# The first MLP's second product, issued two slices behind its first product

## The chip, the cores and the metric

The kernel runs on one core of one Trainium2 chip. The metric is the device time of one execution in microseconds (us). A core has five engines that run their own instruction queues in order: TensorE (PE; its weight loads are listed apart as PEld), VectorE (DVE), ScalarE (ACT), GpSimd (POOL) and SyncE (SP, which here issues the DMAs). They meet only through semaphores.

## The reference

Attention reads between `x` (8 batches, 8 heads, 512 rows, 64 columns) and 32 state rows per head, in both directions; the result, 4352 rows of 512, goes through two MLPs, 512 to 2048 to 512, one after the other.

```python
def _moe_ref(x, w_in, w_out, alpha):
    h = x @ w_in
    g = np.maximum(h, 0.0) + alpha * np.minimum(h, 0.0)
    return (g @ w_out).astype(np.float32)

def _moe2_ref(x, w_in, w_out):
    h = x @ w_in
    g = h - np.tanh(h)
    return (g @ w_out).astype(np.float32)
```

## The kernel before, in words

Every fp32 operand of a product is kept as two parts, a high one and the remainder, and a product is three matmuls (high x high, high x low, low x high). The program is written out by hand: the order of the calls in the Python code is the order in each engine's queue.

The first MLP takes the rows in nine blocks: block 0 to block 7 are the batches (512 rows each), block 8 holds the 256 state rows. Its hidden dimension of 2048 is cut into 16 slices of 128 (`f`). A *visit* is one slice of one block. The visits go: block 0, slices 0 to 7; block 1, all 16; block 0, slices 8 to 15; then blocks 2, 3, 4, 5, 6, the state block, and block 7. Within a visit:

- `emit_h` (L614) is the first product: 12 matmuls of 512 columns in block 0, 12 of 256 in the state block, 6 of 512 in the others (there it works from projected states, `ps_p`, L406, two projections a visit in parts of the run). It writes a PSUM bank `ps_h`.
- The activation is four instructions that alternate between two engines: ACT `t` (L621), DVE on `ps_h` (L622), ACT `g` high part (L623), DVE `g` low part (L627). `g` and `t` have two buffers each.
- `emit_o` (L642) is the second product of the slice before (`pend`): 12 matmuls into four PSUM banks `acc` that stay open over a block. At a block's last slice `finish` copies them out (ACT L667, DVE L669).

Other work is hung into a visit at five places by a table `plan`: "early" (after the first product), "gap" (after the start of the activation), "mid", "late" (after the second product) and "end". That is the attention of the next blocks, the projections, the conversion of the first MLP's weights (visits of block 0 and 1; DVE L114, L116, L119, ACT L111, L123 and casts, POOL), the combination of the second MLP's weights (`c_` names, blocks 3 to the state block), and loads. Four PSUM banks `ps_a` are shared by `ps_h`, the projections and the attention's transposes and scores; the pool gives out a bank whose tile has had its last reader. After the first MLP come the second's two products (L832, L1013).

Of the kernel before, what the change touches and what calls it, by code (L numbers as in the profile page):

```python
# [13 lines left out]
F32R = mybir.dt.float32r  # L14
# [8 lines left out]
P = 128  # L23
# [12 lines left out]
def attention_and_two_mlps(ctx, tc, x, state, w1_in, w1_out, alpha, w2_in, w2_out, out):  # L36
    nc = tc.nc
    B, H, S, D = x.shape
# [17 lines left out]
    work = tc.alloc_tile_pool(name="work", bufs=2)  # L56
# [39 lines left out]
    def w_out(f, part):  # L96
        return WO[f // FQ][:, part, f % FQ, :]
# [245 lines left out]
    def lead(b):  # L343
        return b if b % 2 or b == B - 1 else b - 1
# [259 lines left out]
    def emit_h(blk, n, f):  # L604
        ps = ps_a.tile([P, S], F32, tag="a", name="ps_h")
        if 0 < blk < B:
            col = slice(f % FQ * P, (f % FQ + 1) * P)
            pairs = [([PW[blk, f // FQ, g][i][:, col] for i in range(2)], X[0, blk, g]) for g in range(NG)]
        else:
            w = [WS[f][:, i] if blk else w_in(f, i) for i in range(2)]  # L610
            pairs = [([w[i][:, cc, :] for i in range(2)], X[0, blk, cc]) for cc in range(NCC)]
        for k, (w, xt) in enumerate(pairs):
            for m, (i, j) in enumerate(TERMS):
                nc.tensor.matmul(ps[:, :n], lhsT=w[i], rhs=xt[:, j, :n], start=(k == 0 and m == 0),  # L614
                                 stop=(k == len(pairs) - 1 and m == 2))
        return ps[:, :n]

    def act_a(n, f, ph):
        g = work.tile([P, 2, S], F32R, tag="g", name="g")
        t = work.tile([P, S], F32, tag="t", name="t")[:, :n]  # L620
        nc.scalar.mul(t, ph, slope[:, f:f + 1])  # L621
        nc.vector.scalar_tensor_tensor(ph, ph, sign[:, f:f + 1], t, op0=ALU.mult, op1=ALU.max)  # L622
        nc.scalar.mul(g[:, 0, :n], ph, sign[:, f:f + 1])  # L623
        return g

    def act_b(n, f, ph, g):
        nc.vector.scalar_tensor_tensor(g[:, 1, :n], ph, sign[:, f:f + 1], g[:, 0, :n].bitcast(F32),  # L627
                                       op0=ALU.mult, op1=ALU.subtract)

    accs = {}  # L630

    def emit_o(blk, n, f, g):
        w = [w_out(f, i) for i in range(2)]
        first, last = f == 0, f == NF - 1
        if blk == 0:
            first, last = first or f == NF // 2, last or f == NF // 2 - 1
        if first:
            accs[blk] = [ps_acc.tile([P, S], F32, tag="acc", name="acc") for _ in range(NCC)]
        acc = accs[blk]
        for t in range(NCC):  # L640
            for k, (i, j) in enumerate(TERMS):
                nc.tensor.matmul(acc[t][:, :n], lhsT=w[i][:, t * P:(t + 1) * P], rhs=g[:, j, :n],  # L642
                                 start=(first and k == 0), stop=(last and k == 2))
        if last:
            finish(blk, n, acc)
# [9 lines left out]
    def finish(blk, n, acc):  # L655
        for t, a in enumerate(acc):
            if blk == 0 and half_sum:
                y = half_sum[t]
                nc.vector.tensor_tensor(y, a, y, op=ALU.add)
                stores.append((blk, t, y))  # L660
                continue
            if t < 2:
                y = work.tile([P, S], F32, tag="y", name="y")[:, :n]
            else:
                y = work.tile([P, S], F32, tag="sc" if t == 2 else "at", name="y", bufs=1)[:, :n]
            if t % 2 == 0:
                nc.scalar.copy(y, a[:, :n])  # L667
            else:
                nc.vector.tensor_copy(y, a[:, :n])  # L669
            stores.append((blk, t, y))  # L670
# [3 lines left out]
    def store():  # L674
        for blk, t, y in stores:
            nc.sync.dma_start(out=y_dram[blk][t], in_=y)
        stores.clear()
# [366 lines left out]
    def at(i, f, when, *todo):  # L1044
        plan.setdefault((i, f, when), []).extend(todo)
# [28 lines left out]
    with tc.manual_schedule():  # L1074
# [12 lines left out]
        def halves(i, f, *places):  # L1087
            for k, place in enumerate(places):
                at(i, f, place, (conv_step_a, conv_step_b)[k % 2])
# [25 lines left out]
        for b in range(2, B):  # L1115
            for g in range(NG):
                i, f = (0, 0) if b == 2 else (b - 2, 6 + 7 * g) if b == lead(b) else (b - 2, 1 + g)
# [18 lines left out]
        for i, (blk, n) in enumerate(seq):  # L1136
            if 1 < blk < B:
                for q in range(NF // FQ):
                    at(*((i - 1 if i > 2 else 0, 12, "late") if q == 0 else (i, 4 * q - 4 + (i == 2 and q == 1), "early")),
                       partial(load_parts, blk, q))  # L1140

        for i, (blk, n) in enumerate(seq):
# [50 lines left out]

        for f in range(NF // 2):
            halves(0, f, "late", "end")
        pend = None
        visits = [(0, f) for f in range(NF // 2)] + [(1, f) for f in range(NF)] + [(0, f) for f in range(NF // 2, NF)]
        visits += [(i, f) for i in range(2, len(seq)) for f in range(NF)]
        for i, f in visits:
            blk, n = seq[i]  # L1200
            ph = emit_h(blk, n, f)
            for z in plan.get((i, f, "early"), ()):
                z()
            g = act_a(n, f, ph)
            for z in plan.get((i, f, "gap"), ()):
                z()
            if i < B:
                act_b(n, f, ph, g)
            for z in plan.get((i, f, "mid"), ()):
                z()  # L1210
            if i == B:
                act_b(n, f, ph, g)
            if pend:
                emit_o(*pend)
            for z in plan.get((i, f, "late"), ()):
                z()
            pend = (blk, n, f, g)
            for z in plan.get((i, f, "end"), ()):
                z()
            store()  # L1220
        emit_o(*pend)
        store()

        w_outs.release()
# [116 lines left out]
```

## Time and profile before

| what | value |
|---|---|
| median of 3 runs | 1490.14 us (1488.76 to 1491.17) |
| the profiled execution | 1494.99 us, its span 1493.2 us |
| PE busy | 1418.0 us (95%) |
| DVE, ACT, POOL busy | 988.2 (66%), 728.8 (49%), 533.8 us (36%) |
| mean granted TensorE clock | 0.984 |
| L642 matmuls, 1728 | 420.7 us busy, 24.1 us idle before them, 14.8 of it ended by ACT g L623 |
| L614 matmuls, 600 with projected states | 156.9 us busy |

A row of a timeline reads: start, duration, engine, line, operation, output<-input, count, and in brackets the idle time before it with what ended it. A matmul's duration overlaps the next one's, so the step from one group to the next is shorter than its busy time. The first MLP's visits run from 27.66 us to about 803 us of the span. By the starts of the first products, block 1 begins at 105.28, block 2 at 261.39, block 3 at 362.39, the state block at 676.08 and block 7 at 736.84 us.

### The profile page before, as it was taken

The page shows a single profiled execution, that of the slowest core. Times are in us where ns is not written, and L with a number is a line of the kernel's source. Part 1 is how long each engine was busy: PE and PEld are TensorE (multiplying, and loading weights), DVE is VectorE, ACT ScalarE, POOL GpSimd, SP SyncE. Part 2 cuts the span into 40 slices and gives each one's busy share as a digit, 9 for nine tenths or more (in the row PEclk, how much of TensorE's full clock was granted, in tenths as well). Part 3 has the DMA queues.
Part 4 walks back from the last instruction along what each step waited for, and adds up shares of the span by engine and source line. Part 5 has one row for each costly group of instructions (what it writes and reads, how often), then busy time and mean ns, then how long its engine had stood idle before and what let it go on. Part 6 is the DMA issues. An engine that isn't in the chain of part 4 may idle for free.

```text
span 1493.2 us, 22867 instructions
## 1 busy us (share of the span) xinstructions
PE 1418.0 (95%) x8188; PEld 1191.7 (80%) x8188; DVE 988.2 (66%) x1430; ACT 728.8 (49%) x1322; POOL 533.8 (36%) x414
## 2 busy tenths in 40 slices
PE   5869899999899999999999999999999999999998
PEld 2647678777677677778887787877978999999998
DVE  7988755566677576666345555566348698878884
ACT  4656543444555555555334545455245354444443
POOL 2645310000354444446100122222017486666662
PEclk9989999999999999999999999999999999999999
DMA  6446537986677786769855765462986834444321
GB/s 162 133 136 176 142 110 278 314 259 177 185 186 227 205 249 193 227 184 300 247 167 198 250 232 195 141 255 92 318 309 231 309 124 135 141 135 142 135 86 36
DMA packets 227906, 288.12 MB, mean 193 GB/s; under 512 B 57808, under 2 KB 133584, under 8 KB 226768
## 3 DMA queue, kind: packets, MB, share of 16 engines
q1 hardware_dynamic: 227792, 286.66, 60.1%
q8 instruction: 64, 1.05, 0.3%
q14 instruction: 50, 0.41, 0.1%
HBM read 166.54 MB, written 117.96 MB: 191 GB/s over the span
## 4 chain that ended last, share of the span: by engine, by line
PE 70%; DVE 8%; DMA 6%; ACT 4%; issue 3%; SPq 1%; POOL 1%; DVEq 0%; ACTq 0%; POOLq 0%
PE ps_m L1013 21%; PE ps_m L832 17%; PE acc L642 16%; PE ps_h L614 9%; PE ps_p L406 2%; DVE ps_h L622 2%; PE ps_m L897 2%; DVE g L627 2%; DMA gt<-g 1%; DMA c_raw<-in_moe_w_in 1%; ACT g L623 1%; ACT t L621 1%; DMA g<-t 1%; DVE c L849 1%; PE ps_s L503 1%
## 5 line engine op out<-in xcount | busy, mean ns | idle before, releaser
L642 PE MATMUL acc<-g,wo 128*128 128x512 f32 (+1 forms) x1728 | 420.7, 391 | 24.1 <-ACT g L623 14.8
L642 PEld LDWEIGHTS acc<-g,wo 128*128 128x128 f32 x1728 | 314.5, 192 | 108.8 <-ACT g L623 20.0
L1013 PE MATMUL ps_m<-wp,s 128*128 128x256 f32 x2856 | 343.9, 283 | 2.1 <-ACT e L996 2.0
L1013 PEld LDWEIGHTS ps_m<-wp,s 128*128 128x128 f32 x2856 | 342.7, 191 | 3.4 <-ACT e L996 2.3
L832 PE MATMUL ps_m<-x,ch 128*128 128x512 f32 x1344 | 312.4, 394 | 6.3 <-DVE c L849 4.5
L832 PEld LDWEIGHTS ps_m<-x,ch 128*128 128x128 f32 x1344 | 251.9, 188 | 66.4 <-DVE c L849 6.4
L958 DVE TENSOR_TENSOR s<-gt,s 128x512 fp32r<-128x512 f32 (+1 forms) x216 | 221.1, 1075 | 44.5 <-ACT s L974 43.5
L622 DVE SCALAR_TENSOR_TENSOR ps_h<-ps_h,sign,t 128x512 f32<-128x512 f32 (+1 forms) x144 | 104.7, 727 | 145.4 <-ACT t L621 144.8
L623 ACT ACTIVATE g<-ps_h,sign 128x512 fp32r<-128x512 f32 (+1 forms) x144 | 95.8, 665 | 163.6 <-DVE ps_h L622 163.6
L974 ACT CAST s<-gt 128x512 fp32r<-128x512 f32 (+1 forms) x216 | 120.4, 597 | 89.3 <-PE ps_m L1013 37.4
L614 PE MATMUL ps_h<-x,pw 128*128 128x512 f32 x600 | 156.9, 397 | 0.0
L627 DVE SCALAR_TENSOR_TENSOR g<-ps_h,sign,g 128x512 fp32r<-128x512 f32 (+1 forms) x144 | 102.6, 712 | 60.9 <-ACT g L623 57.9
L621 ACT ACTIVATE t<-ps_h,slope 128x512 f32<-128x512 f32 (+1 forms) x144 | 95.7, 665 | 87.6 <-PE ps_h L614 86.9
L843 POOL TENSOR_TENSOR t<-c,t 128x512 f32<-128x512 f32 x32 | 41.7, 1302 | 249.7 <-ACT t L842 226.4
L614 PEld LDWEIGHTS ps_h<-x,pw 128*128 128x128 f32 x600 | 111.0, 189 | 24.2
L236 POOL TENSOR_TENSOR c_q<-c_m,c_q 128x512 int32<-128x512 int32 x32 | 42.1, 1316 | 241.4 <-ACT c_q L123 191.8
L842 ACT ACTIVATE t<-c 128x512 f32<-128x512 f32 x96 | 60.5, 632 | 124.0 <-DVE c L849 112.1
L849 DVE TENSOR_TENSOR c<-ps_m,c 128x512 f32<-128x512 f32 x96 | 64.8, 685 | 56.4 <-PE ps_m L832 47.8
L263 POOL TENSOR_TENSOR c_o<-c_q,c_o 128x512 fp32r<-128x512 f32 (+1 forms) x48 | 54.4, 1134 | 109.7 <-ACT c_o L261 109.7
L843 DVE TENSOR_TENSOR t<-c,t 128x512 f32<-128x512 f32 x64 | 53.9, 843 | 46.6 <-ACT t L842 44.4
L940 POOL TENSOR_TENSOR s<-gt,gt 128x512 f32<-128x512 f32 (+1 forms) x36 | 54.3, 1517 | 85.0 <-DMA gt<-g 83.6
L166 POOL TENSOR_TENSOR cq<-cm,cq 128x512 int32<-128x512 int32 x32 | 41.9, 1311 | 102.3 <-DVE cm L119 64.7
(142 smaller groups left out, 1659.0 us busy)
## 6 DMA issues: line engine op xcount, KB each, us to landing
g<-t SPq DMA_DIRECT2D x128, 256.0 KB, 2.3
gt<-g SPq DMA_DIRECT2D x64, 512.0 KB, 4.9
wc<-c_o SPq DMA_DIRECT2D x112, 256.0 KB, 3.2
ch<-wc SPq DMA_DIRECT2D x56, 512.0 KB, 6.9
pw<-pw SPq DMA_DIRECT2D x96, 256.0 KB, 5.2
wp<-wc SPq DMA_DIRECT2D x28, 512.0 KB, 7.8
xr<-in_x SPq DMA_DIRECT2D x64, 128.0 KB, 3.3
raw<-in_moe_w_in SPq DMA_DIRECT2D x16, 512.0 KB, 3.8
```

Source lines behind the costliest of these rows:

```text
L614: nc.tensor.matmul(ps[:, :n], lhsT=w[i], rhs=xt[:, j, :n], start=(k == 0 and m == 0), stop=(k == len(pairs) - 1 and m == 2))
L621: nc.scalar.mul(t, ph, slope[:, f:f + 1])
L622: nc.vector.scalar_tensor_tensor(ph, ph, sign[:, f:f + 1], t, op0=ALU.mult, op1=ALU.max)
L623: nc.scalar.mul(g[:, 0, :n], ph, sign[:, f:f + 1])
L627: nc.vector.scalar_tensor_tensor(g[:, 1, :n], ph, sign[:, f:f + 1], g[:, 0, :n].bitcast(F32), op0=ALU.mult, op1=ALU.subtract)
L642: nc.tensor.matmul(acc[t][:, :n], lhsT=w[i][:, t * P:(t + 1) * P], rhs=g[:, j, :n], start=(first and k == 0), stop=(last and k == 2))
L832: nc.tensor.matmul(b, lhsT=w[p][:, cc], rhs=XT[key, i][cc][:, q], start=(i not in GOES_ON and cc == k == 0), stop=(cc == 1 and k == 2), sk ...
L843: eng.tensor_tensor(t, h, t, op=ALU.subtract)
L849: nc.vector.tensor_tensor(h, ps[j, i], h, op=ALU.add)
L958: nc.vector.tensor_tensor(made[k - 1][:, 1], src, made[k - 1][:, 0].bitcast(F32), op=ALU.subtract)
L974: nc.scalar.copy(made[k][:, 0], source(blk, i, jj))
L1013: nc.tensor.matmul(dst[:, t * HW:(t + 1) * HW], lhsT=s[:, p, r, t * P:(t + 1) * P], rhs=w[:, q], start=first, stop=(jj == NJ // 2 - 1 and ...
```

## The change

`emit_o` now runs for the slice before the last one: `pend` is a queue, and in visit f the second product of slice f-2 is issued. The allocation of `g` and its high part move out of `act_a` into `act_b`, behind "gap", "mid" and the second product. `g` keeps two buffers, so g(f) takes the buffer that the second product of f-2, issued just before, has read. Line numbers shift by one: L621, L622, L623, L627 of before are L620, L621, L625, L626 after. One load of projected states of block 2 moves from visit 1 to visit 2 of that block.

```diff
     def act_a(n, f, ph):
-        g = work.tile([P, 2, S], F32R, tag="g", name="g")
         t = work.tile([P, S], F32, tag="t", name="t")[:, :n]
         nc.scalar.mul(t, ph, slope[:, f:f + 1])
         nc.vector.scalar_tensor_tensor(ph, ph, sign[:, f:f + 1], t, op0=ALU.mult, op1=ALU.max)
+
+    def act_b(n, f, ph):
+        g = work.tile([P, 2, S], F32R, tag="g", name="g")
         nc.scalar.mul(g[:, 0, :n], ph, sign[:, f:f + 1])
-        return g
-
-    def act_b(n, f, ph, g):
         nc.vector.scalar_tensor_tensor(g[:, 1, :n], ph, sign[:, f:f + 1], g[:, 0, :n].bitcast(F32),
                                        op0=ALU.mult, op1=ALU.subtract)
+        return g
...
-                    at(*((i - 1 if i > 2 else 0, 12, "late") if q == 0 else (i, 4 * q - 4 + (i == 2 and q == 1), "early")),
+                    at(*((i - 1 if i > 2 else 0, 12, "late") if q == 0 else (i, 4 * q - 4 + 2 * (i == 2 and q == 1), "early")),
...
-            g = act_a(n, f, ph)
+            act_a(n, f, ph)
             for z in plan.get((i, f, "gap"), ()):
                 z()
-            if i < B:
-                act_b(n, f, ph, g)
             for z in plan.get((i, f, "mid"), ()):
                 z()
-            if i == B:
-                act_b(n, f, ph, g)
-            if pend:
-                emit_o(*pend)
+
+            if len(pend) == 2:
+                emit_o(*pend.popleft())
+            pend.append((blk, n, f, act_b(n, f, ph)))
             for z in plan.get((i, f, "late"), ()):
                 z()
-            pend = (blk, n, f, g)
             for z in plan.get((i, f, "end"), ()):
                 z()
             store()
-        emit_o(*pend)
+        while pend:
+            emit_o(*pend.popleft())
```

On PE, near the end of block 6, before: a first product, the second product of the slice before it (`g_6395` is made from `ps_h_6388`, the next rows show), a first product.

```order
L614 MATMUL ps_h_6431<-x0_6_0_5355,pw_6197 128x512 x3
L614 MATMUL ps_h_6431<-x0_6_1_5690,pw_6200 128x512 x3
L642 MATMUL acc_5867<-g_6395,wo3_903 128x512 x3
L642 MATMUL acc_5868<-g_6395,wo3_903 128x512 x3
L642 MATMUL acc_5869<-g_6395,wo3_903 128x512 x3
L642 MATMUL acc_5870<-g_6395,wo3_903 128x512 x3
L614 MATMUL ps_h_6467<-x0_6_0_5355,pw_6197 128x512 x3
```

The same visit on PE now: the second product takes `g_6364`, which is made from `ps_h_6311`, the slice before `ps_h_6376`.

```order
L614 MATMUL ps_h_6419<-x0_6_0_5343,pw_6185 128x512 x3
L614 MATMUL ps_h_6419<-x0_6_1_5678,pw_6188 128x512 x3
L642 MATMUL acc_5892<-g_6364,wo2_1255 128x512 x3
L642 MATMUL acc_5893<-g_6364,wo2_1255 128x512 x3
L642 MATMUL acc_5894<-g_6364,wo2_1255 128x512 x3
L642 MATMUL acc_5895<-g_6364,wo2_1255 128x512 x3
L614 MATMUL ps_h_6455<-x0_6_0_5343,pw_6185 128x512 x3
```

The products themselves and their number are unchanged; the second is one slice further back.

On ACT, the two visits before that one, before: `t`, the high part `g`, then other work. What each instruction waits for stands in brackets.

```order
L621 ACTIVATE t_6331<-ps_h_6323,slope_92 128x512 [waits PE_49,Activation_49]
L623 ACTIVATE g_6330<-ps_h_6323,sign_91 128x512 [waits DVE_49]
L123 ACTIVATE c_q_6364<-c_raw_6188 128x512
L336 CAST x0_7_1_6379<-at_6335 128x512 [waits DVE_49]
L261 CAST c_o_6386<-c_s_6275 128x512 [waits DMAHW7_49,Pool_49]
L621 ACTIVATE t_6396<-ps_h_6388,slope_92 128x512 [waits PE_49,Activation_49]
L623 ACTIVATE g_6395<-ps_h_6388,sign_91 128x512 [waits DVE_49]
```

The same on ACT now:

```order
L620 ACTIVATE t_6318<-ps_h_6311,slope_92 128x512 [waits PE_49,Activation_49]
L123 ACTIVATE c_q_6349<-c_raw_6176 128x512
L625 ACTIVATE g_6364<-ps_h_6311,sign_91 128x512 [waits DVE_49,PE_49]
L336 CAST x0_7_1_6367<-at_6321 128x512 [waits DVE_49]
L261 CAST c_o_6374<-c_s_6263 128x512 [waits DMAHW7_49,Pool_49]
L620 ACTIVATE t_6383<-ps_h_6376,slope_92 128x512 [waits PE_49,Activation_49]
L625 ACTIVATE g_6403<-ps_h_6376,sign_91 128x512 [waits DVE_49,PE_49]
```

The high part now stands behind the visit's "gap" and "mid" work (here `c_q`), and waits for PE as well as for DVE.

At the very start on PE (visits 1 and 2), both in one piece: a second product left out between two transposes.

```order
-L537 MATMUL ps_e<-ident,e_441 128x128 x4
-L642 MATMUL acc<-g,wo_389 128x512 x12
+L537 MATMUL ps_e<-ident,e_439 128x128 x4
 L537 MATMUL ps_e<-ident,e_451 128x128 x4
 L614 MATMUL ps_h<-x_0_0_347,wi_339 128x512 x3
```

Every second product comes one visit later, so two of them follow the last first product where one did.

## Rows read from the trace of the kernel before

**Rows 1.** Stretches: us, busy of PE, PEld, DVE, ACT, POOL (count), PEclk, DMA share, GB/s.

```profile
28.00:105.00 77.00, 59.65 (x357) 43.87 (x358) 66.43 (x117) 48.11 (x93) 41.95 (x32) 0.93 0.51 142
105.00:184.00 79.00, 69.14 (x299) 52.10 (x289) 63.51 (x94) 47.30 (x85) 35.74 (x27) 0.94 0.58 162
184.00:344.00 160.00, 156.78 (x780) 121.81 (x779) 93.03 (x171) 72.07 (x131) 3.81 (x3) 0.99 0.68 229
344.00:674.00 330.00, 316.63 (x1651) 244.03 (x1650) 221.60 (x375) 179.80 (x320) 137.63 (x134) 0.99 0.72 207
674.00:736.00 62.00, 56.25 (x405) 52.22 (x404) 30.77 (x52) 28.09 (x60) 26.49 (x26) 0.94 0.96 284
```

**Rows 2.** Waits of PE from 344 to 674: us in total, times, longest.

```profile
PE acc L642 <- ACT g L623: 8.7, 8, 3.9
PE acc L642 <- DVE g L627: 4.1, 11, 0.7
```

**Rows 3.** Waits of PE from 674 to 736.

```profile
PE acc L642 <- ACT g L623: 3.4, 4, 1.4
PE ps_h L614 <- DVE x L337: 2.0, 2, 1.2
```

**Rows 4.** Waits of PE from 28 to 184.

```profile
PE ps_h L614 <- DVE g L627: 4.4, 3, 3.8
...
PE acc L642 <- DVE g L627: 3.3, 3, 1.9
...
PE acc L642 <- ACT g L623: 2.8, 2, 1.7
```

**Rows 5.** Waits of PE from 184 to 344.

```profile
PE ps_p L406 <- DVE g L627: 1.8, 1, 1.8
```

**Rows 6.** Timeline: one activation that nothing else holds up.

```profile
522.63 1.53 PE L614 MATMUL ps_h<-x,pw 128*128 128x512 f32 x6
...
524.26 0.69 ACT L621 ACTIVATE t<-ps_h,slope 128x512 f32<-128x512 f32 x1 [0.26 <-PE ps_h L614]
...
524.99 0.76 DVE L622 SCALAR_TENSOR_TENSOR ps_h<-ps_h,sign,t 128x512 f32<-128x512 f32 x1 [0.29 <-ACT t L621]
525.78 0.69 ACT L623 ACTIVATE g<-ps_h,sign 128x512 fp32r<-128x512 f32 x1 [0.83 <-DVE ps_h L622]
...
526.50 0.75 DVE L627 SCALAR_TENSOR_TENSOR g<-ps_h,sign,g 128x512 fp32r<-128x512 f32 x1 [0.76 <-ACT g L623]
```

**Rows 7.** Timeline around the longest of the waits of rows 2.

```profile
371.52 1.52 PE L614 MATMUL ps_h<-x,pw 128*128 128x512 f32 x6
...
373.98 3.02 PE L642 MATMUL acc<-g,wo 128*128 128x512 f32 x12
376.84 1.52 PE L614 MATMUL ps_h<-x,pw 128*128 128x512 f32 x6
377.47 0.67 ACT L111 ACTIVATE c_m<-c_raw 128x512 f32<-128x512 f32 x1 [6.20 <-DMA c_raw<-in_moe_w_in]
...
380.02 0.69 ACT L621 ACTIVATE t<-ps_h,slope 128x512 f32<-128x512 f32 x1
...
382.28 0.49 PE L642 MATMUL acc<-g,wo 128*128 128x512 f32 x1 [3.92 <-ACT g L623]
```

**Rows 8.** Stretches around three waits for `g`, columns as in rows 1.

```profile
380.00:390.00 10.00, 7.43 (x24) 5.76 (x25) 5.75 (x11) 5.66 (x11) 4.55 (x5) 0.83 0.45 94
496.00:506.00 10.00, 7.78 (x29) 5.65 (x28) 6.89 (x12) 5.49 (x10) 3.23 (x3) 0.83 0.41 141
676.00:690.00 14.00, 11.14 (x53) 8.93 (x52) 10.55 (x14) 6.30 (x15) 7.33 (x7) 0.76 0.90 278
```

**Rows 9.** Timeline of PE: a projection of block 1 and slice 8.

```profile
144.73 0.86 PE L406 MATMUL ps_p<-wi,snp 128*128 128x512 f32 x3
145.43 1.53 PE L614 MATMUL ps_h<-x,wo 128*128 128x512 f32 x6
...
155.34 5.06 PE L642 MATMUL acc<-g,wo 128*128 128x512 f32 x11 [1.88 <-DVE g L627]
160.20 1.05 PE L614 MATMUL ps_h<-x,wo 128*128 128x512 f32 x2
```

**Rows 10.** Timeline of SP: that projection's load back.

```profile
154.41 1.12 SPq L422 DMA_DIRECT2D wo<-pe  x2
```

**Rows 11.** DMA issues, 105 to 184: count, KB each, us to landing.

```profile
wo<-pe SPq DMA_DIRECT2D x4, 128.0 KB, 2.2
```

More of the change, by code (lines that the diff above doesn't have):

```diff
@@ L1195, in attention_and_two_mlps @@
             halves(0, f, "late", "end")
-        pend = None
+        pend = deque()
         visits = [(0, f) for f in range(NF // 2)] + [(1, f) for f in range(NF)] + [(0, f) for f in range(NF // 2, NF)]
```

## The prediction

> **What bounds the kernel now.** I read the stretches first, for where PE is not busy, then PE's waits in each, then the timeline around the longest. PE is the bound nearly everywhere, but not evenly. From 344 to 674, 67 visits, it is busy for 316.63 of 330 us at a clock of 0.99 [rows 1], and of the 13.4 us left 8.7 + 4.1 = 12.8 us are waits of the second product for `g`, in 19 pieces [rows 2]. In the state block it idles 5.75 us of 62, and its clock is 0.94; 3.4 us are waits for `g`, 2.0 for the block's input [rows 1, 3]. From 28 to 184 it idles 17.35 + 9.86 us, and DVE is nearly full, 66.43 of 77 and 63.51 of 79 us [rows 1]; the waits for `g` in front of the second product are 3.3 + 2.8 = 6.1 us, and 4.4 us more are first products that want a PSUM bank which the low part of an older `g` still reads [rows 4].
>
> Why `g` is late: an activation that nothing holds up ends its high part 2.31 us after the first product (524.16 to 526.47), its low part 3.09 us after it (527.25) [rows 6]. The second product of that slice starts one second product and one first product later: 2.86 us (373.98 to 376.84) [rows 7] plus some 1.4 (1.53 less the overlap with the next group, which is 0.16 us in [rows 9], 0.86 against a step of 0.70). That is 4.3 us if no other PE work stands between, and the spare is 4.3 - 3.1 = 1.2 us. Any instruction that ACT or DVE does or waits for in between uses it up. In the longest wait ACT stood 6.20 us at a conversion that waited for a DMA, with `t` behind it; PE then stood for 3.92 us [rows 7].
>
> **The change, part by part.** No instruction is added or taken away. Three things move.
>
> *The second product is one visit further back.* Now g(f) must be there one further second product and first product later. *The high part waits for the second product of f-2*, since it takes that product's buffer. From the end of that product, by the steps of [rows 6], 0.10 to start, 0.69, 0.03, 0.75: the low part is done 1.57 us after. It is wanted after the next visit's first and second product and the first product of the visit after: 1.4 + 2.86 + 1.4 = 5.7 us. The spare grows from 1.2 to 4.1 us. So of a wait of w us, which was a lateness of w + 1.2, there stays w + 1.2 - 4.1: the 3.92 us become 1.0, and the others in [rows 2] (4.8 us in seven, 4.1 us in eleven of at most 0.7) become nothing, as none but perhaps one of them can be over 2.9 us. I take 0.5 us for what stays, because `t` and the high part no longer stand directly behind each other and ACT can do its "mid" work in between.
>
> What queues behind the new wait: on ACT the "late" and "end" work of the visit and `t` of the next; on DVE the low part, and behind it the same. ACT and DVE must finish a visit's work in a visit's time; in 344 to 674 a visit is 330 / 67 = 4.93 us, DVE works 221.6 / 67 = 3.31 us of it and ACT 2.68 [rows 1], so a hold costs them time that they have.
>
> The Trainium skill, "PSUM — Partial Sum Buffer", section "Engine vs sequencer instructions", says that the queues of ScalarE, VectorE and GpSimdE are strictly first in, first out. The trace agrees: `t` at 380.02 us stood behind ACT's wait of 6.20 us [rows 7]. It speaks against a wait put into ACT's queue in every visit, and is why the first rival below exists.
>
> *Term A, 344 to 674.* Waits 12.8 - 0.5 = 12.3 us. Two of them also let the clock fall: 0.83 over 10 us twice is 1.7 us each [rows 8], 3.4 us in all (one level is 1.2, the other 2.4 GHz; I count the missing share as time, since PE is the bound there). A = -15.7 us; at worst the waits shrink by half with no clock back (-6.4), at best nothing stays (-16.2).
>
> *Term B, the state block.* 3.4 us of waits and (1 - 0.76) x 14 = 3.4 us of clock [rows 3, 8] could go, but the DMA share there is 0.96, which leaves 62 x 0.04 = 2.5 us if its transfers must lie within it [rows 1]. Bounds 0 and -6.8; I take the nearer row, -2.5. The 2.0 us for the input stay.
>
> *Term C, 28 to 184.* In block 1 a projected state reaches its place through a DMA (L422) that waits for stores before it. For slice 8 the last one is issued by 154.41 + 1.12 and lands 2.2 us later, at 157.7 [rows 10, 11]; the first product that wants it started at 160.20, behind a wait of 1.88 us and a second product at the low clock [rows 9]. So the two longest waits of [rows 4], 1.9 + 1.7 us, and their clock bring at most 2.5 us, whatever else goes. Of the other 2.5 us of the 6.1 I take 1.4, since an earlier slice passes through the same chain. Together -3.9. The bank wait of 3.8 us [rows 4] I halve: the copy that frees the bank no longer stands behind ACT's wait for DVE, but DVE itself is full. -1.9. Against it: by the start of block 1 six second products are done where seven were, so one of 2.86 us moves from a stretch in which PE waits for DVE into one in which PE is wanted: +2.9. C = -2.9. From below, DVE's idle time, 10.57 + 15.49 us [rows 1], is all that can go: -26; from above, a hold that costs DVE 0.3 us in each of 20 visits beyond its idle time, +6.0.
>
> *Term D, new bank waits, 28 to 344.* `ps_h` is now read until 1.57 us after the second product. I counted in the new order 23 groups on PE, projections and transposes in visits 3 to 47 mostly, that take this bank before another second product. What lies between is a projection (0.70 us to the next group) and a first product, 2.1 us [rows 9], so the 1.57 us fit, with 0.5 to spare; two of the 23 are first products with some 1.45 us in front. I take 0; the bounds are -1.8 (the wait of [rows 5] goes) and 23 x 0.5 = +11.5, if DVE is as late as half an instruction more each time.
>
> The moved load still lies two visits ahead of its use, `finish` only changes places with the high part, and from 736 on no wait for `g` stands among those above. All 0.
>
> Sum: -15.7 - 2.5 - 2.9 = -21.1 us, on the profiled execution 1494.99 to 1473.9. The median of the runs lies 4.85 us lower, at 1490.14; the same difference gives **1469 us**.
>
> **The rivals.**
>
> *DVE and ACT are held where they are the bound (slower).* From 28 to 184, 20 visits, DVE has 26.06 / 20 = 1.30 us a visit to spare [rows 1]. If the second product starts only when DVE has done its "mid" work, DVE stands for that product and the high part: 2.86 + 0.79 = 3.65 us at most. At a mean of 2.7 the loss is 20 x 1.4 = 28 us; less A and B (18.2) that is +10, 1500 us. It decides against the change from a mean hold of 2.2 us on, where 20 x 0.9 = 18 eats A and B. For it: DVE's fullness. Against it: PE waits for DVE there, so the second product of f-2, whose `g` is a visit old, is mostly over when DVE gets to the low part. 8%.
>
> *The waits move.* Banks, the round trip or `c_raw` loads end last where `g` did: half of D's upper bound (5.8) and A's clock (3.4) are lost, +9: 1478 us. For it: the order puts 23 groups close behind, and DVE was late for one such bank already [rows 5]. 17%.
>
> *More goes.* All of A, B and 15 of C's 26 us: -16.2 - 6.8 - 15 = -38, 1452 us. For it: ACT no longer waits for DVE between `t` and `g`. Against: DMA at 0.96 and the round trip. 10%.
>
> *It does not do what it says.* With two buffers the high part can't start before the second product of f-2 has ended; if late work of ACT and DVE always filled the 4.1 us, `g` would be late as now, 1490 us. The load of 3.31 in 4.93 us speaks against it. 5%.
>
> **How the numbers follow.** My forecast (1458 to 1477) has 60%. I take 1456 to 1485: it leaves out the slower case, no change and half of "more goes", 18%. About 0.2%, 3 us, is what a measurement of this kernel can tell from none. Faster by more: 60 + 17 + 10, less 1 for the tail of the moved waits, 86%. Within: 6%. Slower: 8%.
>
> **What would show it.** Right: waits of the second product for `g` (now L625, L626) near zero from 344 to 736, and the clock of the three stretches of [rows 8] back at 1.0; DVE's idle time in front of the low part, ended by ACT's `g`, grows; in 28 to 184 the stretch is 0 to 6 us shorter. Term D wrong: waits of `ps_p`, `ps_xt` or `ps_h` for the low part of over 3 us in 28 to 344. Term B wrong: first products of the state block that wait for `ws` loads. The whole is wrong if 28 to 184 grows by more than the 18 us that A and B bring.

## The result and the profile after

The changed kernel takes 1476.39 us (median of 4 runs, 1475.17 to 1477.24) against 1489.83 for the kernel before on the same chip: 0.9899 of it, 95% interval 0.9888 to 0.9911. A second measurement gave 1476.38 and 0.9908 (0.9893 to 0.9923). So it is faster by 13 to 14 us, within the range; the likeliest case had 1469.

Both kernels were profiled twice. Cut at the starts of first products (visits counted from 0, in the order in which they run: 48 is block 3, 112 the state block, 128 block 7), the profiles give, in us:

| stretch | before | again | after | again | difference of the means |
|---|---|---|---|---|---|
| start to visit 48 | 362.39 | 362.87 | 355.93 | 356.50 | -6.4 |
| visits 48 to 112 | 313.69 | 312.85 | 300.29 | 299.84 | -13.2 |
| state block | 57.94 | 55.45 | 59.38 | 58.89 | +2.4 |
| block 7 to the first L832 | 67.65 | 67.70 | 69.65 | 69.91 | +2.1 |
| from there to the end | 691.5 | 690.3 | 690.3 | 692.4 | +0.4 |

The sum, -14.7 us, is the difference of the spans. (Block 7 of the first profile begins at 734.02 us. The 736.84 given above is its second visit.)

The same stretches as in [rows 1], by the visits at which they begin and end; then the visits of the three short stretches of [rows 8]; last a second slow spot in the state block. The columns are those of [rows 1]:

```profile
28.00:103.00 75.00, 58.47 (x356) 42.78 (x354) 65.27 (x118) 48.24 (x94) 42.13 (x32) 0.92 0.52 146
103.00:175.00 72.00, 65.64 (x282) 50.16 (x271) 63.29 (x91) 46.26 (x83) 36.22 (x27) 0.95 0.64 177
175.00:336.00 161.00, 157.21 (x780) 120.67 (x779) 92.51 (x170) 73.67 (x132) 3.83 (x3) 1.00 0.68 227
336.00:654.00 318.00, 314.26 (x1657) 243.64 (x1656) 220.47 (x377) 177.27 (x319) 139.15 (x134) 1.00 0.74 213
654.00:714.00 60.00, 54.40 (x382) 50.87 (x381) 28.70 (x51) 27.40 (x58) 26.57 (x26) 0.91 1.01 300
371.20:380.00 8.80, 8.80 (x42) 7.11 (x40) 6.72 (x11) 4.29 (x9) 4.18 (x5) 1.00 1.02 253
483.00:492.00 9.00, 9.00 (x43) 7.30 (x42) 6.16 (x11) 4.30 (x9) 3.52 (x3) 1.00 0.45 150
656.00:672.00 16.00, 12.55 (x52) 9.86 (x51) 10.05 (x17) 8.64 (x18) 9.91 (x10) 0.79 1.00 302
690.00:705.00 15.00, 12.84 (x95) 12.44 (x94) 3.75 (x9) 5.40 (x12) 4.57 (x5) 0.89 1.02 312
```

From 336 to 654, PE idles 3.7 us where it idled 13.4, and where the two long waits of blocks 3 and 4 were the clock is 1.00. At the start of the state block it is 0.79, hardly better than the 0.76 of [rows 8]. PE's waits for the second product's start there (first two lines; [rows 2] had 8.7 and 4.1 for `g`), its waits in the state block (the next three; [rows 3]), and up to visit 48 the first product's for a bank that the low part still reads (the last; [rows 4, 5]); us in total, times, longest:

```profile
PE acc L642 <- DVE g L626: 0.9, 1, 0.9
PE acc L642 <- ACT y L667: 0.6, 1, 0.6
...
PE acc L642 <- ACT g L625: 2.0, 1, 2.0
PE ps_h L614 <- DVE x L337: 1.9, 2, 1.2
PE ps_h L614 <- ACT x L336: 1.5, 1, 1.5
...
PE ps_h L614 <- DVE g L626: 1.7, 2, 1.1
```

The waiting has moved to the engines that have time. The groups of the low and the high part (busy us, mean ns, idle us before them and what ended it):

```profile
L626 DVE SCALAR_TENSOR_TENSOR g<-ps_h,sign,g 128x512 fp32r<-128x512 f32 (+1 forms) x144 | 103.4, 718 | 163.8 <-ACT g L625 163.7
L625 ACT ACTIVATE g<-ps_h,sign 128x512 fp32r<-128x512 f32 (+1 forms) x144 | 95.5, 663 | 179.7 <-PE acc L642 138.9 <-DVE ps_h L621 27.8 <-PE ps_xt L469 7.6
```

ACT now stands 138.9 us for the second product of two slices before; DVE's idle time ahead of the low part grew from 60.9 us. What PE paid for ACT's part of it is asked by a run below.

The state block is longer by 2.4 us. 1.4 of them are work that came in. Counted in the traces, it has 2 second products of 512 columns and 14 of 256 where it had 1 and 15, and block 7 has 2 of 256 columns where it had 1; one of 512 columns steps 2.80 us to the next group, one of 256 columns 1.41. This is the second product that was put off, paid half here and half in block 7. The rest shows in the timeline at the block's start, and at its second slow spot:

```profile
650.28 1.13 SPq L685 DMA_DIRECT2D yl<-xs  x2
...
655.56 0.71 ACT L336 CAST x<-yl 128x256 fp32r<-128x256 f32 x2 [5.37 <-DMA yl<-xs]
...
658.85 0.39 PE L614 MATMUL ps_h<-x,ws 128*128 128x256 f32 x1 [1.52 <-ACT x L336]
660.48 0.72 PE L614 MATMUL ps_h<-x,ws 128*128 128x256 f32 x3 [1.24 <-DVE x L337]
...
697.30 0.40 ACT L261 CAST c_o<-c_q 128x256 fp32r<-128x256 f32 x1 [3.24 <-DMA wc<-c_o]
697.61 0.47 ACT L625 ACTIVATE g<-ps_h,sign 128x256 fp32r<-128x256 f32 x1
...
698.13 3.24 PE L642 MATMUL acc<-g,wo 128*128 128x256 f32 x12 [2.02 <-ACT g L625]
```

Twice ACT stands for a DMA (5.37 and 3.24 us) with a high part queued behind it, and PE waits at the end of that chain; the 12 matmuls at 698.13 then take 3.24 us (the granted clock is 0.50 from 699.1 to 701.2), while the 12 first-product matmuls of the same size at 694.52 took 1.58. That is the pattern of [rows 7], with the DMA queues full (share 1.01).

### The profile page after: what moved, and what is told of

It is laid out like the page before. It is cut to its first block, busy times and chain, and to the rows that moved or that the text cites. A ratio compares the mean times of both kernels' runs of the same rounds, so it can differ in the third digit from the quotient of the medians.

```text
span 1475.5 us, 22886 instructions
## 1 busy us (share of the span) xinstructions
PE 1414.0 (96%) x8188; PEld 1189.1 (81%) x8188; DVE 980.9 (66%) x1430; ACT 727.7 (49%) x1322; POOL 535.4 (36%) x414
## 3 DMA queue, kind: packets, MB, share of 16 engines
q1 hardware_dynamic: 227792, 286.66, 60.9%
## 4 chain that ended last, share of the span: by engine, by line
PE 64%; DVE 7%; ACT 2%; issue 2%; DMA 2%; POOL 1%; SPq 1%; ACTq 0%; DVEq 0%; POOLq 0%
PE ps_m L1013 22%; PE ps_m L832 19%; PE acc L642 13%; PE ps_h L614 7%; PE ps_m L897 2%; DVE ps_h L621 1%; PE ps_p L406 1%; DVE g L626 1%; DMA c_raw<-in_moe_w_in 1%; DVE c L849 1%; DVE c_m L116 1%; DVE c_m L119 1%; ACT g L625 1%; DVE c_m L114 1%; PE ps_s L503 0%
## 5 line engine op out<-in xcount | busy, mean ns | idle before, releaser
L642 PE MATMUL acc<-g,wo 128*128 128x512 f32 (+1 forms) x1728 | 414.7, 389 | 3.6 <-ACT g L625 2.0
L832 PE MATMUL ps_m<-x,ch 128*128 128x512 f32 x1344 | 312.2, 394 | 6.2 <-DVE c L849 4.8
L832 PEld LDWEIGHTS ps_m<-x,ch 128*128 128x128 f32 x1344 | 251.8, 188 | 66.1 <-DVE c L849 6.8
L958 DVE TENSOR_TENSOR s<-gt,s 128x512 fp32r<-128x512 f32 (+1 forms) x216 | 217.8, 1060 | 43.5 <-ACT s L974 42.6
L626 DVE SCALAR_TENSOR_TENSOR g<-ps_h,sign,g 128x512 fp32r<-128x512 f32 (+1 forms) x144 | 103.4, 718 | 163.8 <-ACT g L625 163.7
L625 ACT ACTIVATE g<-ps_h,sign 128x512 fp32r<-128x512 f32 (+1 forms) x144 | 95.5, 663 | 179.7 <-PE acc L642 138.9
L614 PE MATMUL ps_h<-x,pw 128*128 128x512 f32 x600 | 157.7, 398 | 2.3 <-DVE g L626 1.1
L621 DVE SCALAR_TENSOR_TENSOR ps_h<-ps_h,sign,t 128x512 f32<-128x512 f32 (+1 forms) x144 | 104.4, 725 | 65.1 <-ACT t L620 64.4
L614 PEld LDWEIGHTS ps_h<-x,pw 128*128 128x128 f32 x600 | 109.8, 188 | 29.4 <-issue 1.5
L620 ACT ACTIVATE t<-ps_h,slope 128x512 f32<-128x512 f32 (+1 forms) x144 | 95.9, 666 | 56.7 <-PE ps_h L614 56.5
```

The source lines that it names most:

```text
L832: nc.tensor.matmul(b, lhsT=w[p][:, cc], rhs=XT[key, i][cc][:, q], start=(i not in GOES_ON and cc == k == 0), stop=(cc == 1 and k == 2), sk ...
L958: nc.vector.tensor_tensor(made[k - 1][:, 1], src, made[k - 1][:, 0].bitcast(F32), op=ALU.subtract)
```

## The experiments

Two theories stood at the start. *Distance*: a `g` that may be one visit late takes the waits away. *Place*: ACT no longer stands between `t` and the high part waiting for DVE, and the distance is idle. Each run but the second profile of the kernel before was timed in five rounds against the kernel before on the same chip. The first number is the ratio with its 95% interval; stretches are those of the table above.

**Place without distance.**

```diff
-            if len(pend) == 2:
+            if len(pend) == 1:
```

> The changed kernel with one second product outstanding instead of two: the high and low part keep their new place behind the mid work, but the second product is one visit behind its first product, as before. Distance theory (a g that may be one visit late is what took the waits away): the spare is 1.2 us as before, less the mid work of ACT and DVE that now stands in front of the high part, so the waits of the second product for g in blocks 3 to 6 stay at 12 us or grow; 1490 us or more, up to 1510. Place theory (ACT no longer stands between t and g waiting for DVE, the distance is idle): those waits are under 3 us and the time is that of the changed kernel, 1476 us.

1.0067 (1.0053 to 1.0081), 1502.58 us. Visits 48 to 112 take 326.97 us. PE's waits there:

```profile
PE acc L642 <- ACT g L625: 11.0, 10, 3.2
PE acc L642 <- DVE g L626: 6.6, 18, 0.6
```

17.6 us where before has 12.8. In blocks 3 to 6 the place does harm by itself, since the mid work eats the spare of 1.2 us; the distance is worth 26.9 us from there (326.97 to 300.07). The place theory is refuted for these blocks. But visit 48 comes at 357.94, 4.7 us before that of the kernel before: there the place helps.

**Distance two from block 3 on, and only up to block 2.** The other visits run at distance one, with the high and low part behind the gap work, in front of the mid work.

```diff
+            two = i > 2          # the other run: i < 3
+            if not two:
+                while len(pend) > 1:
+                    emit_o(*pend.popleft())
+                if i < B:
+                    g = act_b(n, f, ph)
```

> Blocks 0 to 2 in the order of before, distance two and the new place from block 3 on (visit 48). Theory that the gain is the waits of blocks 3 to 6 (13.4 us between the two profiles, or some 9 if the profiled run of before was slow by the 4.85 us it lies above its median), less 1.4 us in the state block: 1478 to 1482 us, with waits for g in blocks 3 to 6 under 3 us. Rival, that most of the gain is that of blocks 0 and 1 (7.5 us there): 1484 us or more.

> The complement: distance two and the new place in blocks 0 to 2, the order of before from block 3 on; at block 3's first visit two second products follow each other. Theory that blocks 0 and 1 gain by themselves (the waits there gone; 4.6 us of the 7.5 up to visit 20, and 2.9 us that only moved a second product to later): 1485 to 1487 us. Rival, that the 7.5 us are only a second product done later plus waits that come back: 1489 to 1491 us. Waits for g in blocks 3 to 6 are again 9 to 13 us by both.

From block 3: 0.9916 (0.9903 to 0.9928); up to block 2: 0.998 (0.997 to 0.999). So most of the gain is that of blocks 3 to 6, 302.99 us in the first run and 314.25 in the second; the 0.998 lies between what theory and rival had for it. The 302.99 hold a saving of 2.9 for the second product that is put off there, and against it a wait for ACT's copy of block 2's result, which stood behind a conversion that waited 6.61 us for its load (the changed kernel waits 0.6 us for that copy):

```profile
PE acc L642 <- ACT y L667: 3.6, 1, 3.6
```

Visit 48 comes at 357.91 in the first run and at 357.17 in the second, 5 us early in both, though only the second has distance two there.

**The high part moved, nothing else.** What both have in common is that the high part has left its place directly behind `t`. The kernel before with that alone:

```diff
     def act_a(n, f, ph):
-        g = work.tile([P, 2, S], F32R, tag="g", name="g")
...
-        nc.scalar.mul(g[:, 0, :n], ph, sign[:, f:f + 1])
-        return g
+    def act_b(n, f, ph):
+        g = work.tile([P, 2, S], F32R, tag="g", name="g")
+        nc.scalar.mul(g[:, 0, :n], ph, sign[:, f:f + 1])
```

> The kernel before with one move: the high part leaves its place directly behind t and stands directly in front of the low part, behind the gap work (in block 7 behind the mid work). Distance one throughout. All runs so far with the high part behind the gap work, at either distance, have visit 48 some 315 us behind visit 2, both profiles of before 320 and 321. Theory that the gain of blocks 0 to 2 is this move and not the distance: 1484 to 1486 us (5.5 us less than before), visit 48 at 315 us behind visit 2, blocks 3 to 6 in 313 to 315 us with 11 to 13 us of waits for g. Rival, that the distance makes it: 1490 us and 320 us.

Visit 48 comes at 357.45 us, as the theory says. The waits of ACT's high part for DVE up to visit 20, in the second profile of before and in this run:

```profile
ACT g L623 <- DVE ps_h L622: 29.6, 20, 5.6
```

```profile
ACT g L625 <- DVE ps_h L621: 10.9, 15, 2.8
```

The time, though, is 0.9994 (0.9982 to 1.0006): no difference, where 1484 to 1486 us was expected. Visits 48 to 112 take 314.66 us and block 7 69.06, each 1.4 us more than before, with no more waiting. This is what led to the last run below.

**Distance two with the high part at its old side of the mid work.**

```diff
-            for z in plan.get((i, f, "mid"), ()):
-                z()
...
             if len(pend) == 2:
                 emit_o(*pend.popleft())
             pend.append((blk, n, f, act_b(n, f, ph)))
+            if i < B:
+                for z in plan.get((i, f, "mid"), ()):
+                    z()
```

> Distance two, but the high and low part at the place of before: behind the gap work and, up to block 7, in front of the mid work, with the second product of two visits back ahead of them. The run with the new place and distance one was 0.7% slower than before (blocks 3 to 6: 327 us against 313.7), so the place by itself costs and the distance gains 26.7 us from there. Theory that at distance two the place costs nothing any more, since the spare of 4.1 us takes it: blocks 3 to 6 in 300 us as in the changed kernel, 1476 us. Rival, that the place still costs a part of its 13 us: 1465 to 1473 us. Second rival, that what was mid work now stands behind the wait for the second product, on PE and in the queues of ACT and DVE, and is late for its own users in blocks 0 and 1: 1480 to 1490 us.

0.997 (0.9957 to 0.9983). Blocks 3 to 6 take 309.20 us, by waits that the changed kernel does not have:

```profile
PE ps_w L592 <- DVE wide L577: 6.0, 5, 1.9
PE ps_e L537 <- ACT e L519: 3.8, 3, 1.6
```

The second rival came true, only in other blocks than it said: PE's own mid work now stands behind the second product, and the attention's chain between PE, DVE and ACT is late for itself. Distance two wants the place behind the mid work.

**Is the hold paid for?** The high part gets a third buffer, so that ACT waits for no second product.

```diff
-        g = work.tile([P, 2, S], F32R, tag="g", name="g")
+        g = [work.tile([P, S], F32R, tag=f"g{k}", name="g", bufs=3 - k) for k in range(2)]
...
-        low[k] = work.tile([P, DM], I32, tag="cq", name="cq", bufs=3)
+        low[k] = work.tile([P, DM], I32, tag="cq", name="cq", bufs=2)
...
-                    work.tile([P, DM], F32R, tag="cq", name="pl", bufs=3))
+                    work.tile([P, DM], F32R, tag="cq", name="pl", bufs=2))
```

> The changed kernel with three buffers for the high part of g and two for the low part (the room comes from the buffers of a step of the weights' conversion, two for three), so that ACT's high part waits for no second product any more; DVE's low part still does. Theory that the hold of ACT, 138.9 us of waits in the profile of the changed kernel, costs nothing because PE is the bound: 1474 to 1478 us, with the waits of ACT for the second product gone. Rival, that ACT's hold of 13 us in the first 175 us is time lost there, as my first rival had it: 1466 to 1472 us. The smaller buffers could cost 1 to 3 us in blocks 0 and 1.

0.9961 (0.995 to 0.9973). ACT's 138.9 us of waits for PE are gone (first line), and visits 48 to 112 still take 300.11 us, visit 32 still comes at 254.83 (changed kernel: 254.16 and 254.71). From visit 48 to 112 ACT's hold costs nothing. Up to visit 32 its end gains nothing either, though there the smaller buffers may hide a gain; and a hold is left on DVE, whose low part now waits 49.7 us for the second product. The loss is in block 2, 109.8 us against 101.8, most likely the price of the room taken from the weights' conversion, whose buffers the projections share (second line, visits 32 to 40):

```profile
L625 ACT ACTIVATE g<-ps_h,sign 128x512 fp32r<-128x512 f32 (+1 forms) x144 | 95.6, 664 | 68.1 <-DVE ps_h L621 68.1
...
PE ps_p L406 <- DVE pl L414: 5.4, 1, 5.4
```

**The state block's input.**

```diff
-                at(i, 13, "mid", partial(load_reads, nn))
+                at(i, 13, "early", partial(load_reads, nn))
...
-                    at(i, *((NF - 1, "early") if cc > 1 else (14, "mid")), partial(split_reads, cc, nn))
+                    at(i, *((NF - 1, "mid") if cc > 1 else (14, "late")), partial(split_reads, cc, nn))
```

> The changed kernel with the state block's load of its input issued before instead of behind the mid work of visit 13, and its conversions by ACT behind g instead of before it (visit 14 late instead of mid, visit 15 mid instead of early). Theory that the state block lost its gain because ACT stands 5.37 us for that load with g behind it: the first waits of the state block (1.52, 1.24, 0.69 us) shrink and the clock there rises; 1473 to 1475 us. Rival, that the block is held by its transfers (DMA share 1.01 to 1.02): the block's time of 59.4 us stays, 1476 us. If the conversions are now late for the first product, its waits grow by 1 to 3 us: 1477 to 1479 us.

0.9885 (0.9868 to 0.9903), 1473.97 us: not to be told apart from the changed kernel. The state block took 57.43 us, 1.7 less, and block 7 71.39, 1.6 more. PE's waits for the input (first and third line) are 3.1 us, as in the second profile of the changed kernel:

```profile
PE ps_h L614 <- DVE x L337: 2.1, 2, 1.3
PE acc L642 <- ACT g L625: 1.8, 1, 1.8
PE ps_h L614 <- ACT x L336: 1.0, 1, 1.0
```

Only half of the edit took effect. The conversions moved, and ACT's wait for the load fell from 5.37 to 2.43 us. The load did not: SyncE issues it behind the same five transfers, the first of which waits 4.2 us for DVE in both runs. Load and first product of the state block, in the kernel before and in this run:

```profile
668.54 1.13 SPq L685 DMA_DIRECT2D yl<-xs  x2
...
676.08 0.98 PE L614 MATMUL ps_h<-x,ws 128*128 128x256 f32 x7
```

```profile
648.80 1.13 SPq L685 DMA_DIRECT2D yl<-xs  x2
...
654.69 0.92 PE L614 MATMUL ps_h<-x,ws 128*128 128x256 f32 x6
```

The load leads by 7.5 us before and by 5.9 here, as in the changed kernel (650.28 to 656.22). Over all 14 traces PE's wait for the input goes with this lead: 2.8 to 3.6 us where it is 5.1 to 6.0, 0.7 to 2.0 where it is 7.5 to 7.8, none where it is 8.7 or more. So the input's lateness goes with its load, and not with the place of its conversion; an earlier load was not tried.

**Distance one from the state block on**, on top of that, and in the second run in blocks 0 and 1 up to visit 20 as well.

```diff
+            far = 2 if i < B - 1 else 1
+            while len(pend) > far:
+                emit_o(*pend.popleft())
             ph = emit_h(blk, n, f)
...
-            if len(pend) == 2:
+            if len(pend) == far:
```

> The kernel with the later conversions of the state block's input, and besides distance two ending with block 6: one waiting second product is issued in front of the state block's first product, where PE waits for that input, and the state block and block 7 run at distance one. Theory that the second product which distance two leaves over at the end costs 2.0 us there and is free where PE waits anyway (3 us of waits for the input): 1471 to 1474 us, block 7 up to the last phase in 67.5 to 69 us. Rival, that the state block at distance one gets its waits for g back (3.4 and 2.4 us in the two profiles of before, 5.3 with the high part behind the mid work): 1475 to 1478 us.

> The same, and distance two starts only at visit 20 (block 1, slice 12), so that the second product which the start of distance two puts off is done while DVE is the bound and PE has room. Theory: visit 20 comes no later than in the changed kernel (134 us behind visit 2), and from there one second product, 2.86 us, is saved: 1468 to 1471 us. Rival, that blocks 0 and 1 need distance two as well: visit 20 comes 2 to 4 us later and it is 1472 to 1476 us. Second rival, that the visit without a second product makes PE wait for DVE there, as at the start of block 3 in the run with distance two from block 3: nothing gained, the time of the run before.

0.9901 (0.9883 to 0.992) and 0.9903 (0.9885 to 0.9922). In the profiles the first reaches L832 from visit 104 in 161.2 us, where the run above takes 163.7, but the medians show no gain. Its wait for the input is gone, with the load 8.7 us ahead, and in the state block its waits for `g` are 3.4 us, as the rival had it. The second reaches visit 20 at 177.57 us (the first: 174.58), about as its first rival had it, and visit 48 at 355.63 (355.10): up to visit 20 distance two is worth about as much as the second product that it puts off, and nothing is left.

**The place of `g` in memory.** In most of block 7 nothing waits, so PE's steps can be read there. A second product and the next first product, in the second profile of before, the run with only the high part moved, and the second profile of after:

```profile
748.01 2.88 PE L642 MATMUL acc<-g,wo 128*128 128x512 f32 x12
750.73 1.52 PE L614 MATMUL ps_h<-x,pw 128*128 128x512 f32 x6
```

```profile
746.35 2.96 PE L642 MATMUL acc<-g,wo 128*128 128x512 f32 x12
749.15 1.54 PE L614 MATMUL ps_h<-x,pw 128*128 128x512 f32 x6
```

```profile
734.69 2.96 PE L642 MATMUL acc<-g,wo 128*128 128x512 f32 x12
737.49 1.54 PE L614 MATMUL ps_h<-x,pw 128*128 128x512 f32 x6
```

The step is 2.72 us in the first and 2.80 in the others. (From the first product, which does not read `g`, to the next second product it is 1.36 and 1.38.) What differs is where `g` lies: in each partition its buffers begin at bytes 87168 and 91264 before, at 88384 and 92480 in the changed kernel, since tiles get their addresses in the order of their first use.

```diff
     def act_a(n, f, ph):
+        if not first_g:
+            first_g.append(work.tile([P, 2, S], F32R, tag="g", name="g"))
...
-        g = work.tile([P, 2, S], F32R, tag="g", name="g")
+        g = first_g[0] if len(first_g) == 1 else work.tile([P, 2, S], F32R, tag="g", name="g")
+        first_g.append(None)
```

> The changed kernel with g's two buffers at the addresses of before, to which the first one is given its place in the first visit ahead of t; the order of all instructions stays. In every kernel whose g is first placed behind the activation's first half, its buffers start 192 or 1216 bytes further, at 64 bytes past a multiple of 128 (87360 or 88384 for 87168), and in block 7, where nothing is waited for, a second product takes PE 2.80 us from its start to the next first product's, in both profiles of before 2.72; in blocks 3 to 6 it is 2.88 against 2.83. Theory that the address of g makes each of its matmuls 3% slower: 2.72 us again in block 7, which ends 1.3 us sooner, blocks 3 to 6 some 64 x 0.05 = 3.2 us sooner, and the same rate in the other blocks; together 144 x 0.05 to 0.08 = 7 to 11 us less than the changed kernel: 1465 to 1470 us. Rival, that the steps come from the order or the distance and not from the address: 2.80 us in block 7 and 1476 us.

0.9877 (0.9858 to 0.9896), 1471.26 us: the fastest median here, some 5 us below the changed kernel's, though the intervals of the ratios still touch. The step is 2.72 us again:

```profile
732.23 2.88 PE L647 MATMUL acc<-g,wo 128*128 128x512 f32 x12
734.95 1.52 PE L614 MATMUL ps_h<-x,pw 128*128 128x512 f32 x6
```

Visits 48 to 112 take 298.42 us, 1.7 less than the changed kernel's mean, the state block 57.39, block 7 68.81, 1.0 less. I had expected 7 to 11 us in all, and the median lies between theory and rival; in blocks 3 to 6 part of it turned into waits of the attention, 1.9 us each for `e2t` and for the low part in front of `ps_xt` (1.3 and 0.9 in the changed kernel).

With 256 columns the address works the other way round. In the state block, in the second profile of before and the second of after, with nothing waiting:

```profile
724.04 1.60 PE L642 MATMUL acc<-g,wo 128*128 128x256 f32 x12
725.48 1.57 PE L614 MATMUL ps_h<-x,ws 128*128 128x256 f32 x12
```

```profile
705.32 1.57 PE L642 MATMUL acc<-g,wo 128*128 128x256 f32 x12
706.73 1.58 PE L614 MATMUL ps_h<-x,ws 128*128 128x256 f32 x12
```

The step is 1.44 us in the first, 1.41 in the second, and 1.44 again in this run. So "3% slower" holds for 512 columns alone.

**Both kernels again.**

> The changed kernel once more, on the chip of the other runs. By the first measurement 0.990 of before; stretches that differ between its two profiles are scatter and not effects: blocks 3 to 6 within 1 us of 300.3; the first 20 visits, the state block and block 7 within 3 us of 148.0, 59.4 and 69.7.

> The kernel before once more, for a second profile. The run that keeps the order of before up to block 2 had its visit 16 at 155.2 us and its visit 48 at 357.9, where the first profile of before has 160.2 and 362.4, with the same instructions. If that profile was a slow one there, this one shows 155 and 358 us again, and blocks 3 to 6 take 313.7 as before; if not, 160 and 362.

They are in the table at the top. After came out as expected. Before shows 362.87 us at visit 48, as its first profile did, so the 5 us by which the other runs are earlier are an effect.

## Why the prediction was right in direction and 7 us off

The forecast was -21.1 us; the profiles give -14.7, the medians -13.4 and -14.4. The range held because it was wide: terms A and B brought 6 us less than forecast.

*The spare, right.* 1.2 us against 4.1: at distance one with the mid work ahead the waits grow to 17.6 us, at distance two 0.9 us stay (forecast 0.5), and DVE idles ahead of the low part instead.

*Term A, right in kind, 2.5 us too large.* Forecast -15.7, measured -13.2. The waits (12.8 to 0.9 for `g`) and the clock came as worked out. The step that failed is "no instruction is added or taken away", taken to mean that none changes its length: the move of the allocation shifted `g`, and each second product became some 0.05 us longer here (2.83 to 2.88 us from its start to the next first product's, the middle of the undisturbed ones). With `g` at its old address the term is 298.42 - 313.27 = -14.9. The rest is of the size of new waits of the attention, 1.3 us for `e2t` and 0.9 for the low part in front of `ps_xt`; that they are the rest is not shown.

*Terms C and D, near in size by luck, and for another reason.* Forecast -2.9, of which +2.9 for the second product that is put off. Measured -6.4 up to visit 48; the second product is paid in the state block and in block 7, +1.4 each, not at the start of block 1. So -3.6. The step that failed is that the two longest waits and their clock "bring at most 2.5 us, whatever else goes", as the load back lands at 157.7. The load is not fixed. It is issued at 147.61, 6.8 us sooner than in [rows 10]:

```profile
147.61 1.12 SPq L422 DMA_DIRECT2D wo<-pe  x2
...
149.89 1.09 PE L614 MATMUL ps_h<-x,wo 128*128 128x512 f32 x3 [0.84 <-DMA wo<-pe]
```

Visit 20 came 8.1 us sooner, where I had 0 to 6 for that stretch; from there to visit 48 1.7 us were lost again (0.7 with `g` at its old address). What gained is the place, not the distance: at distance one the three runs with the high part moved reach visit 48 4.7 to 5.2 us early, and with `g` at its old address it still comes at 353.08, so the address is not the cause. At distance two it is some 2 us more (355.93 and 356.50, and 354.11 and 357.17 in two runs with the same order up to there), less than the 2.8 us of the second product that is still owed. The prediction had this only as a halved bank wait and as the reason for "more goes". Term D's zero holds: up to visit 48 first products wait 1.7 us for the low part, where a projection waited 1.8 [rows 5] and first products 4.4 before [rows 4].

*Term B, wrong.* Forecast -2.5, measured +2.4, of which 1.4 is the second product that was put off. The waits for `g` went from 3.4 to 2.0 us in one place, but the block's input became later (3.4 us for 2.0). The step that failed is "the 2.0 us for the input stay": I did not ask how far ahead of the block its load would start once PE arrived sooner. It led by 7.5 us and leads by 5.9. ACT's conversion of that input now stands in front of a high part and waits 5.37 us for the load. The Trainium skill's "PSUM — Partial Sum Buffer", section "Engine vs sequencer instructions", has the rule, queues strictly first in, first out, and I had weighed it for the new wait alone, not for what now stands in front of the high part. Moving the conversion behind it left the input as late. The other part is the clock, 0.91 over the block in both profiles of after, 0.94 and 0.97 in those of before. The run with distance two from block 3 on has the changed kernel's order here and nearly its waits (4.9 us for 5.4 and 5.2), a clock of 0.97, and took 55.99 us, the changed kernel 59.38 and 58.89; the run with a third buffer took 54.97, also at 0.97. Why the clock falls in one and not in the other stays open.

*Block 7*, taken as 0, is +2.1: 1.4 for its part of the second product that was put off, and some 1.0 for the address of `g`.

*The 4.85 us between the profiled run and the median* I took off at the end. The second profile of before is 4.1 us shorter, 2.5 of it in the state block and 0.8 in A's stretch. So most of the excess lay where terms A and B were read, and this step counted a part of it twice. At the start of the state block, where the first profile has a clock of 0.76 [rows 8], the second has 1.00:

```profile
675.70:689.70 14.00, 11.50 (x78) 10.07 (x77) 10.02 (x16) 6.38 (x14) 8.26 (x8) 1.00 0.94 307
```

The 3.4 us of clock that term B put at stake were not in every execution.

*The rivals.* "DVE and ACT are held where they are the bound": refuted as an outcome, since that stretch became 8.1 us shorter. That the holds cost nothing there is not shown: ACT's was taken away only at the price of smaller buffers, DVE's not at all. "The waits move": its number, 1478, is near the result by luck, for banks did not do it; of its three places only the loads did, in the state block. "More goes": its reason was right in blocks 0 to 2, its size not. "It does not do what it says": refuted.

## What to carry to other kernels

A producer and consumer at distance one fail here at the first late instruction; a second slice of distance pays when the queue that then waits has time to spare, and in blocks 3 to 6 ACT's wait cost nothing. Work that is put off does not vanish: find the stretch in which it is paid before a longer stretch is called a loss. Where an instruction between two engines stands directly behind its half, moving other work in between can help one stretch and harm another, so test the place and the distance apart. After any move of an allocation, compare the length of an undisturbed instruction in both traces: a layout can take back what the order gains.

## What the hardware showed unexpectedly

The rate of the second product's matmuls depended on the address of their moving operand. 12 of them with 512 columns step 2.72 us with `g` at 87168 and 91264, and 2.80 us with `g` at 87360, at 88384 and in the split buffers of the third-buffer run: 3% more, with the same instructions, clock 1.00 and no waits. With 256 columns they step 1.44 and 1.41 us, so the address that is slower for the one width is faster for the other. The first two addresses are multiples of 128 and the others lie 64 past one; that this is the reason was not tried. A few small tiles of DVE moved along with `g`, and back with it, but DVE uses none of them in the stretches of block 7 that are shown. The Trainium skill's "SBUF — State Buffer", section "Operand start alignment", asks only for a multiple of the element size and says that it speaks of legality and not of speed; all these addresses keep its rule.
